# First batch's attention issued from one hand-kept list, with small matmuls ahead of the first MLP

## The chip, the cores and the metric

The kernel runs on one NeuronCore of a Trainium2 chip. The metric is device microseconds (us) of one execution. Five engines with queues of their own work on it: TensorE (PE in the profile, its weight loads PEld), VectorE (DVE), ScalarE (ACT), GpSimd (POOL) and SyncE (SP), which here only issues DMAs. DMAs are issued from the queues of SP, ACT and POOL.

## The reference

Eight batches, 12 heads, 448 positions, 64 elements per head. Attention with normalised queries and keys, then a LayerNorm and an MLP with a residual:

```
q_n, k_n = rmsnorm(q, g_q), rmsnorm(k, g_k)          # over the 64 elements of a head
attn = softmax(q_n @ k_n.T / sqrt(64));  o = attn @ v # [8, 12, 448, 64]
x = o.transpose(0, 2, 1, 3).reshape(8, 448, 768)
xn = (x - mean) / sqrt(var + 1e-6) * g_ln
out = x + relu(xn @ w_ch1) @ w_ch2                    # 768 -> 3072 -> 768
```

All inputs and the output are float32.

## The kernel before, in words

**Stages.** Two heads make a *pair*; a batch has six pairs (p = 0 to 5 in batch 0). Batch 0's attention runs first and alone; then each batch's MLP runs on PE with the next batch's attention cut into small steps between its matmuls (`run`, L560). So only the first attention, with the LayerNorm behind it, has no MLP beside it.

**Units.** q, k and v are loaded and prepared in *units* (L23). Batch 0 has four: unit 0 is pair 0, unit 1 pair 1, unit 2 pairs 2 and 3, unit 3 pairs 4 and 5; unit 4 is the first of batch 1. `prep_ops` (L173) gives the pieces of a unit's preparation, which go over 448 elements per partition for one pair and 896 for two:
- `sk`, `sq`: squares of k and q on ACT (L198); `tk`, `tq`: their sums on DVE (L201)
- `root`: the reciprocal square root of the sums (`_rsqrt`, L47): an addition on DVE (L51), a first guess by an exponential on ACT (L54), then two Newton steps of three tiny DVE instructions each (L57 to L59). `rootq` and `rootk` do one half
- `kg`: k times the product of the two gains, on POOL (L207); `khi`: its float16 part, on POOL for units 1 to 3 (L213), else on ACT (L215); `klo`: the rest, on DVE (L218)
- `qn`, `qdup`: the scaled q in float16 on DVE (L66), and its second copy on DVE (L225) or, for units 2 and 3, POOL
- `vmain`, `vleft` (or `vall`): v in float16, on POOL (L231, L237)

**Per pair.** `trans_k` transposes k on PE into the PSUM tile `tr` and DVE copies it out (L267); `trans_q` does the same for q through the same `tr`, copied out by ACT for pairs 1, 3 and 5 (L281) and by DVE for the others (L283). `scores(p, i)`, i = 0 to 6, are one or two matmuls (L296 to L300) and an exponential on ACT (L302), with two PSUM buffers between. `values(p, i)` are four small matmuls (L325, L327); the last calls `evac_o`, four DVE instructions (L340 to L347). `stats` are the LayerNorm's partial statistics on DVE (L459), every second pair.

**Between attention and MLP.** `ln_ops(0)` (L462): three aggregations (L474), three normalisations `norm` (L479), the LayerNorm's `root`, then for three tiles of tokens a transpose on PE (`ln_trans`, L505) and a copy to `xnT` by ACT (L508, first two) or DVE (L510, third). `run` puts one step of unit 4's preparation after each of these four pieces. The MLP's first matmul is `up` (L523), in 24 chunks of six matmuls and one ReLU on ACT (L525); the second half is `down` (L534).

**Order.** PE, ACT, POOL and SP take their instructions in the order in which the program emits them (`manual_schedule`, L778); on DVE a scheduler decides. What is emitted when in batch 0 comes from `FIRST_ORDER` (L29), rows of (step, unit, pieces): steps -2 and -1 lie ahead of the first scores, step 7p+i goes with `scores(p, i)`; values and transposes of the next pair are spread over the steps by a fixed rule (L398 to L425).

**Loads.** `load_first` (L129) issues q of pair 0 from SP and k of pairs 0 and 1 from ACT's queue, then the rest from SP, with v of pairs 0 and 1 ahead of pairs 2 to 5 of q and k. The weights go from POOL's queue: three parts of w1 (L433) after step 1, two halves of w2 (L438) at step 21.

Of the kernel before, what the change touches and what calls it, by code (L numbers as in the profile page):

```python
# [26 lines left out]
EXP_BIAS = -4.0  # L27

FIRST_ORDER = [  # L29
    (-2, 0, "begin", "sq", "sk", "kg", "tq", "rootq", "tk", "khi", "qn", "qdup", "klo", "rootk"),  # L30
    (-2, 1, "begin", "sk", "sq", "kg", "tk", "tq", "khi"),
    (-1, 1, "root", "klo", "qn", "qdup"),
    (-1, 2, "begin", "sk", "kg", "sq", "tk", "khi"),
    (0, 1, "vall"),
    (0, 2, "tq"), (2, 2, "root"), (4, 2, "klo"), (5, 2, "qn", "qdup"),
    (7, 3, "begin", "sk", "kg"), (9, 3, "sq"), (10, 2, "v"),
    (11, 3, "tk", "khi"), (12, 3, "tq"), (13, 3, "root"), (15, 3, "klo"), (17, 3, "qn", "qdup"),
    (19, 3, "v"),
]
# [7 lines left out]
def _rsqrt(nc, out, a, t, eps, last=None, mul=1.0):  # L47

    eng = nc.vector
    if mul == 1.0:  # L50
        eng.tensor_scalar(out=a, in0=a, scalar1=eps, scalar2=None, op0=ALU.add)  # L51
    else:
        eng.tensor_scalar(out=a, in0=a, scalar1=mul, scalar2=eps, op0=ALU.mult, op1=ALU.add)  # L53
    nc.scalar.activation(out, a.bitcast(INT32), AFT.Exp, scale=-0.5 * LN2 * 2.0 ** -23,  # L54
                         bias=0.5 * LN2 * (127.0 - 0.043))
    for i in range(2):
        eng.tensor_tensor(out=t, in0=out, in1=out, op=ALU.mult)  # L57
        eng.scalar_tensor_tensor(out=t, in0=t, scalar=-0.5, in1=a, op0=ALU.mult, op1=ALU.mult)
        eng.scalar_tensor_tensor(out=last if i and last is not None else out, in0=t, scalar=1.5,  # L59
                                 in1=out, op0=ALU.add, op1=ALU.mult)  # L60

# [13 lines left out]
class _Fast:  # L75
# [53 lines left out]
    def load_first(self):  # L129
        nc = self.nc  # L130
        flat = self.hT.rearrange("p f n -> p (f n)").bitcast(FP32)
        t = [flat[:, 2688 * n:2688 * n + 2688].rearrange("p (w g d) -> p w g d", w=NPAIR, d=D)
             for n in range(2)]
        v = self.p_in.tile([128, 3, 14, D], FP32, tag="qkv", name="vfirst")
        t.append(v.rearrange("p n g d -> p (n g d)").rearrange("p (w g d) -> p w g d", w=NPAIR,
                                                               d=D))
        main = lambda eng, n, p: self.load_main(eng, n, t[n][:, p, 0:6], 0, 2 * p, 2)
        left = lambda eng, n: self.load_left(eng, n, t[n][:, :, 6], 0, 0, H)
        for eng, n in ((nc.sync, 0), (nc.scalar, 1)):
            main(eng, n, 0)  # L140
            left(eng, n)
        main(nc.scalar, 1, 1)
        for n, p in ((0, 1), (2, 0), (2, 1)):
            main(nc.sync, n, p)
        left(nc.sync, 2)
        for p in (2, 4):
            for n in (1, 0):
                for i in range(2):
                    main(nc.sync, n, p + i)
        for p in range(2, NPAIR):  # L150
            main(nc.sync, 2, p)
        self.v_first = t[2]
        for u, (b, hs, m) in enumerate(UNITS):
            if b == 0:
                self.loads[u] = [x[:, hs // 2:hs // 2 + m].rearrange("p w g d -> p (w g) d")
                                 for x in t]
# [16 lines left out]
    def prep_ops(self, u):  # L173
# [28 lines left out]

        def root(n=slice(0, 2)):
            _rsqrt(nc, c["rr"][:, n], c["ssq"][:, n], c["rt"][:, n], D * 1e-6, c["rf"][:, n])
# [6 lines left out]
        def khi():  # L211
            if 0 < u < 4:
                nc.gpsimd.tensor_copy(out=c["khl"][:, :, 0], in_=c["t"][1])  # L213
            else:
                nc.scalar.activation(c["khl"][:, :, 0], c["t"][1], AFT.Identity)  # L215
# [8 lines left out]
        def qdup():  # L224
            (nc.gpsimd if 1 < u < 4 else nc.vector).tensor_copy(out=c["qn"][:, :, 1],  # L225
                                                            in_=c["qn"][:, :, 0])
# [14 lines left out]
        def vall():  # L241

            nonlocal v16, vl, p0
            v16, vl, p0 = self.v16[:, 0:2], self.vl[:, 0:2], 0
            vmain()
            vleft()

        if UNITS[u][0] == 0:
            return dict(begin=begin, sk=lambda: square(1), sq=lambda: square(0), kg=kg, khi=khi,
                        tk=lambda: total(1), tq=lambda: total(0), root=root, klo=klo, qn=qn,  # L250
                        rootk=lambda: root(1), rootq=lambda: root(0), qdup=qdup, vall=vall,
                        v=lambda: (vmain(), vleft()))
        return [lambda: (begin(), square(1), kg()), lambda: total(1), lambda: square(0),
                lambda: (total(0), vmain()), khi, root, klo, None, qn, qdup, vleft]
# [14 lines left out]
    def trans_q(self, p):  # L269
# [3 lines left out]
        ps = self.tr[:, 128:128 + 2 * S].rearrange("p (e s) -> p e s", e=2)  # L273
# [6 lines left out]
        if p in (1, 3, 5):  # L280
            nc.scalar.copy(out=qT, in_=ps.rearrange("p e s -> p (e s)"))  # L281
        else:
            nc.vector.tensor_copy(out=qT, in_=ps.rearrange("p e s -> p (e s)"))  # L283
# [67 lines left out]

    def attention(self):
# [3 lines left out]
        prep = [self.prep_ops(u) for u in range(4)]  # L356

        def at(step, u, *names):
            todo.setdefault(step, []).extend(prep[u][x] for x in names)

        for x in FIRST_ORDER:
            at(*x)
# [10 lines left out]
        todo.setdefault(18, []).append(lambda: self.load_unit(5))  # L373
        todo.setdefault(1, []).append(lambda: [self.load_w1(c, c + 1024) for c in range(0, FF, 1024)])
        todo.setdefault(21, []).append(lambda: [self.load_w2(g) for g in range(2)])
        steps, mark = [], []

        def first():
            self.load_first()
            nc, sh = self.nc, self.sh  # L380
            nc.scalar.activation(sh.warm, sh.ones, AFT.Exp)
            for op in todo.pop(-2):
                op()
            self.trans_k(0)
            self.trans_q(0)
            for op in todo.pop(-1):
                op()
            nc.sync.dma_start(sh.gln, self.g_ln.unsqueeze(0).broadcast_to([128, DM]))
            nc.vector.tensor_scalar(out=sh.gln, in0=sh.gln, scalar1=XS, scalar2=None, op0=ALU.mult)
            self.load_unit(4)  # L390

        def batch(b):
            self.xs[b] = self.p_x.tile([128, 3, DM], FP32, tag="x", name="x")
            if b % 2 == 0:
                self.xls[b // 2] = self.p_xl.tile([128, DM], FP32, tag="xl", name="xl")

        steps.append([first])
        for p in range(n + 1):  # L398
            if p == nb0:
                for x in ((0, 1), (2, 3, 4), (5, 6)):  # L400
                    steps.append([lambda i=i: self.values(nb0 - 1, i) for i in x])
                steps[-1].append(lambda: self.stats(nb0 - 1))
                mark.append(len(steps))
                steps += [[op] for op in self.prep_ops(UNIT_PAIR.index(nb0)) if op is not None]
                steps[-1].append(lambda: self.load_unit(6))
                steps += [[lambda: self.trans_k(nb0)], [lambda: self.trans_q(nb0)]]
            for i in range(7):
                c = []
                if i == 0 and p < n and p % NPAIR == 0:
                    c.append(lambda b=p // NPAIR: batch(b))  # L410
# [3 lines left out]
                if p > 0 and p != nb0:  # L414
                    for x in {0: (), 1: (0, 1)}.get(i, (i,)):
                        c.append(lambda p=p, x=x: self.values(p - 1, x))
                if p > 1 and i == 1 and (p - 1) % NPAIR:
                    c.append(lambda p=p: self.stats(p - 2))
                if p + 1 < n and p + 1 != nb0:
# [42 lines left out]
    def ln_ops(self, b):  # L462
# [23 lines left out]
        def first():  # L486
            aggregate()
            for t in range(3):
                norm(t)
            root()  # L490
# [6 lines left out]
        return [first] + [lambda t=t: trans(t) for t in range(n)]  # L497
# [62 lines left out]
    def run(self):  # L560
        steps, mark = self.attention()
        self.pos = 0

        def upto(target):
            while self.pos < min(target, len(steps)):
                for call in steps[self.pos]:
                    call()
                self.pos += 1

        upto(mark[0])  # L570
        for op in self.ln_ops(0):
            op()
            upto(self.pos + 1)
# [167 lines left out]
def kernel(  # L741
# [35 lines left out]
    with ExitStack() as fctx:  # L777
        with tc.manual_schedule(engines={ENG.PE, ENG.Activation, ENG.Pool, ENG.SP}):  # L778
            _Fast(fctx, tc, sh, q, k, v, moe_g_ln, moe_w_ch1, moe_w_ch2, out).run()
# [34 lines left out]
```

## Time and profile before

| | us |
|---|---|
| median of 8 runs (lowest, highest) | 663.51 (662.71, 664.22) |
| the profiled execution | 663.75 |
| its span | 661.9 |
| PE busy in the span | 618.4 |
| DVE, ACT, POOL busy | 377.3, 358.3, 92.5 |
| first transpose of k (L262) | 12.45 |
| first exponential of scores (L302) | 18.56 |
| last matmul of batch 0's values begins (L327) | 53.48 |
| first matmul of the first MLP (L523) | 62.19 |
| last matmul of the last MLP ends (L534) | 654.69 |

The times in the lower half are starts (or the end) in us from the span's beginning. The profiled execution is 1.9 us longer than its span. A profile row gives an instruction's start, its duration, the engine, the line, the operation with the tiles it writes and reads, and in brackets how long its engine had stood idle and what released it. PEclk, or "granted clock", is the share of full speed that TensorE's clock had.

### The profile page before, as it was taken

To read this page: it belongs to the slowest core of one execution; us is meant where nothing else is said; L and a number is where in the kernel's file an instruction comes from. 1 tells how busy PE (TensorE), PEld (TensorE's weight loads), DVE (VectorE), ACT (ScalarE), POOL (GpSimd) and SP (SyncE) were. 2 spreads that over 40 slices of the span, in tenths; PEclk is the share of its full clock that TensorE was granted. 3 is DMA by queue.
4 is the path that set the end of the run, shared out by engine and by line. 5 is a ranking of instruction groups with operands and counts; after the bars stand their busy time and mean duration, and the time that the engine had idled before them with its cause. 6 is when DMAs were issued, how large, how long until landed. Compare 5 with 4: busy or idle time off the path is not lost.

```text
span 661.9 us, 12501 instructions
## 1 busy us (share of the span) xinstructions
PE 618.4 (93%) x5066; PEld 380.7 (58%) x5066; DVE 377.3 (57%) x890; ACT 358.3 (54%) x641; POOL 92.5 (14%) x113
## 2 busy tenths in 40 slices
PE   0676999999999999999999999999999999999995
PEld 0453566655566666655566666655566666654563
DVE  5878778855556566765456666865356553380011
ACT  2694787547843477527754377617764287304300
POOL 2732222120220201201220012202201020000000
PEclk9997999999999999999999999999999999999998
DMA  7999944042030433032130241112331100010011
GB/s 208 244 216 214 222 139 110 4 156 83 3 108 25 130 87 85 25 103 73 41 108 25 83 132 53 58 58 77 83 85 50 48 2 1 25 49 1 0 49 51
DMA packets 71824, 54.81 MB, mean 83 GB/s; under 512 B 22736, under 2 KB 65744, under 8 KB 71760
## 3 DMA queue, kind: packets, MB, share of 16 engines
q1 hardware_dynamic: 61600, 43.86, 22.6%
q0 software_dynamic: 8528, 9.44, 8.4%
q8 instruction: 41, 0.67, 0.4%
q10 hardware_dynamic: 1632, 0.66, 0.4%
q14 instruction: 23, 0.19, 0.1%
HBM read 52.36 MB, written 11.01 MB: 96 GB/s over the span
## 4 chain that ended last, share of the span: by engine, by line
PE 83%; DVE 8%; ACT 4%; DMA 2%; issue 1%; SPq 1%; ACTq 0%; DVEq 0%
PE psH L523 31%; PE psC L534 30%; PE psS L296 7%; PE oA L325 4%; PE tr L278 2%; PE tr L265 2%; DVE xn L479 2%; ACT E L302 2%; PE oB L327 1%; PE psS L299 1%; PE psS L300 1%; PE psX L505 1%; DVE stat L459 1%; DMA hT<-in_k_dram 1%; DMA hT<-in_q_dram 1%
## 5 line engine op out<-in xcount | busy, mean ns | idle before, releaser
L302 ACT ACTIVATE E<-psS,rr_all 128x448 f16<-128x448 f32 x336 | 208.4, 634 | 80.5 <-PE psS L296 65.3
L523 PE MATMUL psH<-xnT,w 128*128 128x512 f16 (+1 forms) x1152 | 247.2, 355 | 1.8 <-ACT xnT L508 1.8
L534 PE MATMUL psC<-w,hT 128*128 128x384 f16 x1344 | 241.5, 326 | 1.9 <-DVE x L538 1.9
L525 ACT ACTIVATE hT<-psH 128x384 f16<-128x384 f32 (+1 forms) x192 | 104.7, 545 | 117.3 <-PE psH L523 114.8
L534 PEld LDWEIGHTS <-hT 128*128 128x128 f16 x1344 | 125.0, 98 | 73.1 <-issue 2.4
L523 PEld LDWEIGHTS <-w 128*128 128x128 f16 x1152 | 106.3, 98 | 86.7 <-issue 5.7
L296 PE MATMUL psS<-qT,kT 128*128 128x448 f16 x288 | 103.0, 360 | 7.7 <-ACT E L302 5.7
L207 POOL TENSOR_TENSOR qkv<-qkv,gprod 128x896 f32<-128x896 f32 x21 | 43.8, 2084 | 418.2 <-issue 301.8
L325 PEld LDWEIGHTS <-E 128*128 128x128 f16 x1008 | 72.1, 98 | 49.6 <-issue 3.9
L538 DVE SCALAR_TENSOR_TENSOR x<-psC,rs_all,x 128x384 f32<-128x384 f32 x48 | 29.5, 615 | 74.8 <-PE psC L534 74.4
L325 PE MATMUL oA<-v,E 128*128 128x65 f16 x864 | 67.3, 194 | 0.0
L267 DVE COPY kT<-tr 128x960 f16<-128x960 f16 x48 | 31.5, 655 | 45.2 <-PE tr L265 44.6
L327 PE MATMUL oB<-v,E 128*128 128x65 f16 x288 | 52.3, 194 | 0.0
L283 DVE COPY qT<-tr 128x896 f16<-128x896 f16 x45 | 28.0, 623 | 35.4 <-PE tr L278 35.0
L296 PEld LDWEIGHTS <-kT 128*128 128x128 f16 x288 | 28.5, 100 | 22.6 <-issue 3.6
L340 DVE RECIPROCAL rec_all<-oA 128x6 f32<-128x6 f32 x48 | 9.4, 196 | 55.2 <-PE oA L325 55.1
L201 DVE TENSOR_REDUCE ssq<-qn 128x14 f32<-128x896 f32 (+1 forms) x25 | 26.2, 1046 | 11.7 <-ACT qn L198 10.6
L327 PEld LDWEIGHTS <-E 128*128 128x128 f16 x336 | 32.6, 97 | 0.1
L218 DVE TENSOR_TENSOR khl<-qkv,khl 128x896 f16<-128x896 f32 x21 | 22.9, 1093 | 16.4 <-ACT khl L215 16.2
L54 ACT ACTIVATE stat<-stat 128x3 f32<-128x3 int32 (+1 forms) x8 | 1.7, 209 | 50.8 <-DVE stat L53 50.8
L201 DVE TENSOR_REDUCE ssq<-khl 128x14 f32<-128x896 f32 (+1 forms) x25 | 26.1, 1046 | 4.3 <-ACT khl L198 3.6
L342 DVE TENSOR_TENSOR x<-oA,rec_all 128x384 f32<-128x384 f32 x48 | 26.8, 558 | 1.5
(89 smaller groups left out, 540.0 us busy)
## 6 DMA issues: line engine op xcount, KB each, us to landing
out_dram<-x SPq DMA_DIRECT2D x24, 384.0 KB, 2.3
qkv<-in_k_dram SPq DMA_DIRECT2D x21, 384.0 KB, 3.3
qkv<-in_q_dram SPq DMA_DIRECT2D x21, 384.0 KB, 3.9
qkv<-in_v_dram SPq DMA_DIRECT2D x21, 384.0 KB, 4.4
w<-in_moe_w_ch_dram POOLq DMA_DIRECT2D x3, 1536.0 KB, 17.7
w<-in_moe_w_ch_dram POOLq DMA_DIRECT2D x2, 2304.0 KB, 32.3
out_dram<-xl SPq DMA_DIRECT2D x8, 192.0 KB, 3.2
qkv<-in_k_dram SPq DMA_DIRECT2D x42, 32.0 KB, 3.3
```

The lines of the kernel that those rows point to most:

```text
L201: nc.vector.tensor_reduce(out=c["ssq"][:, n], in_=c["sq", n], axis=AX.X, op=ALU.add)
L207: nc.gpsimd.tensor_tensor(out=c["t"][1], in0=c["t"][1], in1=sh.gprod.unsqueeze(1).broadcast_to([128, g, D]), op=ALU.mult)
L267: nc.vector.tensor_copy(out=kT.rearrange("p g d -> p (g d)"), in_=ps[:, 0:960])
L283: nc.vector.tensor_copy(out=qT, in_=ps.rearrange("p e s -> p (e s)"))
L296: nc.tensor.matmul(ps[:, 0:S], kT[:, 192 + 128 * i:320 + 128 * i], qT[:, h * S:(h + 1) * S], start=True, stop=True)
L302: nc.scalar.activation(out=c["E"][:, i], in_=ps[:, 0:S], func=AFT.Exp, scale=self.rr[:, 1, g:g + 1], bias=EXP_BIAS)
L325: nc.tensor.matmul(oA[:, t, cs], E[:, i, ts(t, 128)], rhs, start=(i == 0 and t == 0), stop=(i == 6 and t == 2))
L327: nc.tensor.matmul(oB[:, cs], E[:, i, 320:448], rhs, start=(i == 0), stop=(i == 6))
L523: nc.tensor.matmul(ps[:, 0:N], sh.w1[:, dc, ts(f, 128)], xnT[:, dc, 0:N], start=(dc == 0), stop=(dc == NDC - 1))
L525: nc.scalar.activation(out=hT[:, f, 0:N], in_=ps[:, 0:N], func=AFT.Relu)
L534: nc.tensor.matmul(ps[:, 0:384], hT[:, f, ts(t, 128)], sh.w2[:, f, ts(g, 384)], start=(f == 0), stop=(f == NFF - 1))
L538: nc.vector.scalar_tensor_tensor(out=x[:, ts(g, 384)], in0=ps[:, 0:384], scalar=self.rs[:, b, t:t + 1], in1=x[:, ts(g, 384)], op0=ALU.mult ...
```

## The change

1. `FIRST_ORDER` and the step rule for batch 0 are replaced by `ORDER`, one list of pieces for all of batch 0, emitted by `first_attention`. In an entry the first letter is the piece and the last digit the unit: b begin, c and a the squares of q and k, e and d their sums, f the addition, g the guess, h the Newton steps (fq/fk, gq/gk, hq/hk: one half), i kg, j khi, k klo, l qn, m qdup, v the copies of v. K, Q, T are `trans_k`, `trans_q` and `stats` of a pair; S and V are `scores` and `values`; L loads a unit, W a part of the weights, G loads the LayerNorm's gain and G2 scales it.
2. Until the LayerNorm of batch 0 is emitted, DVE too follows the program's order; afterwards its scheduler decides again.
3. `_rsqrt` is split into addition, guess and Newton steps, which stand apart in the list.
4. `trans_q` of batch 0 uses PSUM buffers of its own (`psQ`, from the three that the MLP uses) and no longer `tr`; ACT copies pair 0, DVE pairs 1 to 5 (before: ACT 1, 3, 5). `qdup` of unit 2 moves from POOL to DVE.
5. `load_first` issues everything from SP, in the order q, k of pair 0, then q and k up to pair 3, then v.
6. After batch 0's values, 22 matmuls of 384 columns into an unused tile `psW`. In `ln_ops(0)` the `root` goes behind the transposes, and unit 4's preparation is no longer put between its pieces: it starts inside the first MLP.

From the later part of the first MLP on, the order of instructions on every engine is that of before.

```diff
+WARM = 22
+POOL_HI, POOL_DUP, ACT_Q = (1, 2, 3), (3,), (0,)
+ORDER = """
+b0 c0 e0 fq0 gq0 a0 hq0 i0 d0 fk0 gk0 j0 b1 c1 a1 i1 l0 m0 k0 hk0 d1 K0 e1 j1 Q0 f1 S0.0 g1 h1
+k1 l1 m1 b2 a2 i2 G L4 W0 c2 S0.1 v0 S0.2 d2 K1 S0.3 j2 Q1 S0.4 W1 S0.5 W2 e2 S0.6 f2 g2 h2
+V0.0 S1.0 k2 l2 m2 S1.1 b3 S1.2 a3 S1.3 i3 V0.1 V0.2 V0.3 v2 K2 S1.4 V0.4 S1.5 Q2 c3 V0.5 S1.6
+V0.6 S2.0 T0 S2.1 e3 d3 V1.0 V1.1 S2.2 V1.2 j3 S2.3 V1.3 V1.4 f3 g3 V1.5 S2.4 K3 h3 Q3 k3 S2.5
+l3 S2.6 V1.6 v3 m3 L5 G2 S3.0 S3.1 V2.0 K4 V2.1 W3 S3.2 S3.3 V2.2 V2.3 S3.4 V2.4 Q4 S3.5 V2.5
+S3.6 V2.6 K5 S4.0 S4.1 T1 Q5 V3.0 V3.1 S4.2 V3.2 S4.3 V3.3 S4.4 V3.4 S4.5 V3.5 S4.6 V3.6 S5.0
+V4.0 V4.1 T3 S5.1 S5.2 V4.2 S5.3 V4.3 S5.4 V4.4 W4 S5.5 V4.5 V4.6 V5.0 V5.1 S5.6 V5.2 V5.3
+V5.4 V5.5 V5.6 T5
+""".split()
...
-        for eng, n in ((nc.sync, 0), (nc.scalar, 1)):
-            main(eng, n, 0)
-            left(eng, n)
-        main(nc.scalar, 1, 1)
-        for n, p in ((0, 1), (2, 0), (2, 1)):
+        for n in range(2):
+            main(nc.sync, n, 0)
+            left(nc.sync, n)
+        for n, p in ((1, 1), (0, 1), (1, 2), (1, 3), (0, 2), (0, 3), (2, 0), (2, 1)):
             main(nc.sync, n, p)
         left(nc.sync, 2)
...
-        ps = self.tr[:, 128:128 + 2 * S].rearrange("p (e s) -> p e s", e=2)
+        tr = self.ps_m.tile([128, 1024], FP16, tag="mlp", name="psQ") if p < NPAIR else self.tr
+        ps = tr[:, 128:128 + 2 * S].rearrange("p (e s) -> p e s", e=2)
...
-        if p in (1, 3, 5):
+        if p in ACT_Q:
             nc.scalar.copy(out=qT, in_=ps.rearrange("p e s -> p (e s)"))
...
             for t in range(3):
                 norm(t)
-            root()
+            if b:
+                root()
...
-        return [first] + [lambda t=t: trans(t) for t in range(n)]
+        return [first] + [lambda t=t: trans(t) for t in range(n)] + ([] if b else [root])
...
+        self.first_attention()
+        ps = self.ps_m.tile([128, 512], FP32, tag="mlp", name="psW")
+        for _ in range(WARM):
+            nc.tensor.matmul(ps[:, 0:384], self.sh.id16,
+                             self.v16.rearrange("p s h j d -> p (s h j d)")[:, 0:384],
+                             start=True, stop=True)
         for op in self.ln_ops(0):
             op()
-            upto(self.pos + 1)
...
-        with tc.manual_schedule(engines={ENG.PE, ENG.Activation, ENG.Pool, ENG.SP}):
-            _Fast(fctx, tc, sh, q, k, v, moe_g_ln, moe_w_ch1, moe_w_ch2, out).run()
+        manual = {ENG.PE, ENG.Activation, ENG.Pool, ENG.SP}
+        with tc.manual_schedule(engines=manual | {ENG.DVE}):
+            fast = _Fast(fctx, tc, sh, q, k, v, moe_g_ln, moe_w_ch1, moe_w_ch2, out)
+            fast.run_first()
+        with tc.manual_schedule(engines=manual):
+            fast.run_rest()
```

## The prediction

> **What bounds the kernel now.** I read the busy slices of the page first: PE is at 9 in nearly all of them, and the few low ones lie at the start. The table by stage says the same (columns: window, its length, then busy us of PE, PEld, DVE, ACT and POOL with instruction counts, granted clock, DMA share, GB/s):
>
> ```profile
> 57.70:62.20 4.50, 2.48 (x19) 1.79 (x20) 4.00 (x7) 2.55 (x5) 1.31 (x1) 0.50 1.26 217
> 62.20:66.80 4.60, 4.60 (x15) 2.15 (x15) 4.50 (x8) 2.69 (x5) 2.06 (x4) 0.51 1.32 204
> 66.80:70.00 3.20, 3.20 (x26) 2.06 (x24) 2.76 (x10) 1.50 (x4) 0.00 (x0) 1.00 1.32 205
> 150.00:250.00 100.00, 99.29 (x826) 61.26 (x825) 56.98 (x133) 60.25 (x109) 13.16 (x15) 1.00 0.25 72
> ```
>
> Once the MLPs run, PE is 99% busy. So what the change is worth is the time at which the first MLP matmul starts (62.19 us), plus the clock at which it runs: in the second row 15 matmuls take 4.60 us at clock 0.51, 0.307 each, where six take 0.97 us later (0.162 each).
>
> Second, the chain of waits from the last values to that matmul:
>
> ```profile
> 54.07 0.20 DVE rec_all L340
> ...
> 55.41 1.08 DVE stat L459 x3
> 56.49 0.33 DVE stat L474 x3
> 56.82 2.72 DVE xn L479 x3
> ...
> 59.97 0.69 issue
> 60.65 1.49 ACT xnT L508 x2
> 62.15 0.04 issue
> 62.19 7.26 PE psH L523 x30
> ```
>
> Here see that ACT's two copies end it. They stood behind the LayerNorm's guess (L54, 59.65) and a square of unit 4 (59.80 to 60.75), though their transposes began at 57.74.
>
> Third, what PE waits for in batch 0's attention:
>
> ```profile
> PE tr L262 <- DVE khl L218: 12.4, 1, 12.4
> PE psS L296 <- ACT E L302: 5.2, 9, 2.3
> PE tr L275 <- DVE qn L225: 4.3, 2, 3.0
> ```
>
> DVE and ACT set the pace there, not PE. ACT has 42 exponentials (24.2 us busy, spaced 0.54 when they run back to back), yet they spread from 18.56 to 53.2. DVE is nearly full from 10 to 25 us, and part of that is waiting inside instructions. The timeline shows it, POOL first, DVE below:
>
> ```profile
> 17.31 2.08 POOL L207 TENSOR_TENSOR hT<-hT,gprod 128x896 f32<-128x896 f32 x1 [2.59 <-DMA vfirst<-in_v_dram]
> 17.86 1.56 DVE L58 SCALAR_TENSOR_TENSOR rt<-rt,ssq 128x14 f32<-128x14 f32 x1
> ```
>
> A Newton instruction that takes 0.15 elsewhere takes 1.56 and ends with POOL's kg. The same happened at kg of units 0 and 1 and khi of unit 3: 0.46, 0.95, 1.40 and 0.59 us lost. Sums (L201) and copies out of PSUM beside POOL kept their times (1.07, 0.62).
>
> **The change, part by part.** All against the profiled execution, 663.75 (span 661.9 and 1.85 around it); that is 0.24 above the median.
>
> *Start.* ACT's DMA issue at 6.81 held its table load (7.22) and so the first square to 8.63. Those issues go to SP, so q's square can start when q lands, about 7 us. DVE is held to 7.55 by the gains' product (L766 to L770). From there: sum of q 0.6, addition and guess 0.35, six Newton instructions at 0.20 (1.2), sum of k 0.55, addition 0.16 with 0.4 of holding by kg0: 10.9. Then qn and qdup 0.85, klo 0.6 (12.35); the k half's six Newton steps 1.2 plus 1.05 held by kg1 (1.13 long, starting about 12.7, behind the square of unit 1): 14.65. Sum of unit 1 0.55, copy of kT 0.6: 15.8. q's transposes have their own PSUM and ACT's copy (0.9) is done by then. First exponential 0.57 later (as 17.99 to 18.56): **16.4** instead of 18.56. SP's eighth issue waits for the first landing, as it did before (idle 2.69 to 4.69), so k may land up to 0.7 earlier or later; both ends go into the range.
>
> *Units 1 and 2.* The guess of unit 1 stands on ACT behind the first exponential (16.95), and Newton, klo, qn of unit 1 wait behind it on DVE. The square of k of unit 2 follows that guess, so kg2 starts 1.18 later (18.13), after five Newton steps, and holds the last one, klo and qn until 20.2: 1.85 lost. klo, qn, qdup 1.5; sum 1.0; kT, qT 1.2: 23.85. Sum of q, addition 1.2; the guess of unit 2 comes behind the last exponential of pair 0 at 25.3; Newton 1.55, klo and qn 2.15: 29.0. Here kg3 becomes ready while qn runs, and stands against qdup (0.4), which has moved to DVE. If POOL goes first it costs 2.1, if DVE does, 0. The four kg of before cost 0.46, 0.95, 1.40 and 0, 0.70 on the mean; I take 1.0. qdup, kT, qT 1.6: 31.65, and pair 2's exponentials start at 32.1.
>
> *Units 3 to the end of attention.* On DVE until qT of pair 4: evacuation 1.35, sums 2.0, addition, kT, Newton, qT 2.6, klo and qn 2.1, evacuation, gain, kT, qT 3.0: 42.7. From there ACT sets it: 0.45 to the first exponential, 14 of 0.54 (7.55), 0.35 for the last values: **51.05** instead of 53.70. The copies of qT for pairs 3 and 5 that move to DVE are in this sum (0.55 each); the second (by 47) is hidden by pair 4's exponentials. POOL loses one qdup (0.93). Gain 2.65; with no holding at all 47.5 (then ACT and PE at half clock bound it), with every kg in full 52.7.
>
> *LayerNorm.* Evacuation 1.35 at once (before: 0.37 late, behind pair 4's), statistics 1.0, aggregation 0.33, three norms 2.8, last transpose and DVE's copy 1.05, wake-up 0.05: MLP at 51.05 + 6.6 = 57.65, against 8.49 us from 53.70 to 62.19. ACT's copies are earlier than DVE's now, because guess and squares stand behind them. Gain 1.9. Sum with attention: **4.55**.
>
> *Small matmuls.* 22 of 0.162 are 3.6 us, hidden by the 3.7 until the first norm is done. At half clock they would take 6.8 and delay the transposes by 3.1. Before, clock 0.5 lasted from 56.5 (2.8 after the last matmul) to 66.75. With them, PE is without matmuls other than transposes for about 3.0 us. If the clock stays up, 15 matmuls take 2.44 instead of 4.60: gain **2.15**, otherwise 0. The idle part before the fall was 2.8 without any transposes; 1 us of these lies in the new gap, so I take 2.15.
> [...]
>
> *Unit 4's preparation inside the MLP.* Two squares (0.95 each), two sums (1.07 each), kg now compete with the first ReLUs. First scores of pair 6 come after 10 chunks, not 7. PE idled 1.13 in 70 to 80 for such pieces. From -0.3 (that idling eases) to 1.9 (both squares uncovered): I take **0.4** lost, near the row.
>
> *Weights.* The last part of w1 landed at about 51 (25.4 + 25.6) and is used by the 17th chunk; halves of w2 at 66.8 and 81.6, first used at 103.5. POOL issues w1 at about 20 and 25 now (23.6 before), w2 at about 40: nothing.
>
> Forecast: 663.75 - 4.55 - 2.15 + 0.4 = **657.4**.
>
> **Rivals.**
> 1. *POOL and DVE do not meet.* The order keeps kg beside sums and copies; attention ends at 47.5. For: before, kg3 cost nothing. Against: kg2 follows its square directly. 663.75 - 6.2 - 1.9 - 2.15 + 0.4 = 653.9.
> 2. *The clock falls all the same* in the gap with only transposes. 657.4 + 2.15 = 659.6.
> 3. *The list does not shorten attention* (DVE in fixed order waits for guesses behind exponentials as long as it waited before): end at 53.7, 663.75 - 1.9 - 2.15 + 0.4 = 660.1.
> 4. *Slower: the fixed order on DVE meets all of POOL's work.* POOL has 14.2 us in batch 0 (kg 6.4, khi 2.4, v 4.4, qdup 0.9); I charge 4.3. If the other 9.9 held DVE too, attention would end at 60.95 and the time be 667.3. It is slower by over 0.2% from 7.7 of these 9.9 on. Against it: before, 3.4 of some 15 were lost.
>
> **How the numbers follow.** Chances: forecast 0.45, rival 1 0.17, rival 2 0.20, rival 3 0.10, rival 4 0.08. The forecast alone spans 655.5 to 659.5 (kg3 and its neighbours, landing of k, unit 4). The range to rivals 1 to 3 is 653.3 to 661.5. A measurement of this kernel tells 0.2% (1.3 us) from no change. Faster 0.88: all but rival 4 and the part of rivals 2 and 3 that come together (662.2), which with a small rival 4 gives 0.05 for the same; slower 0.07.
>
> **What would show it.** First exponential near 16.4; DVE instructions of Newton or klo beside kg2 stretched by up to 2 us; the last values ending near 51; first MLP matmul 6.6 later, with the DVE copy ending its wait; clock 1.00 in the first 5 us of the MLP. I am wrong if attention ends after 53.7, if the clock shows 0.5 there, or if PE idles over 2 us in the first ten chunks.

## The result and the profile after

The changed kernel takes 666.09 us (median of 11 executions, 664.66 to 668.18) against 663.50 for the kernel before on the same chip (32 executions): ratio 1.0043 (95% interval 1.0034 to 1.0051). It is **slower** by 2.9 us by the ratio (2.6 by the medians), where 657.4 was forecast. Its profiled execution took 665.45 (span 663.6), 1.70 more than that of before; the sums below go by these two.

| us from the start | before | forecast | after |
|---|---|---|---|
| first exponential | 18.56 | 16.4 | 16.95 |
| first exponential of pair 2 | 34.35 | 32.1 | 35.94 |
| first exponential of pair 4 | 44.39 | 43.15 | 47.82 |
| last values of batch 0 end | 53.70 | 51.05 | 56.51 |
| first MLP matmul | 62.19 | 57.65 | 63.27 |
| first store of the output | 134.00 | | 135.71 |
| last MLP matmul ends | 654.69 | | 656.42 |

Behind the first store (issued when the first MLP is done) the kernels run alike: 520.69 and 520.71 us. The loss arises before it: 1.61 gained at the start, 4.42 lost from the first exponential to the last values, 1.73 gained in the LayerNorm, 0.63 lost in the first MLP.

The table by stage of the changed kernel, the same three stretches as before, shifted with the first MLP matmul (columns: window, length, busy us of PE, PEld, DVE, ACT, POOL, granted clock, DMA share, GB/s):

```profile
58.40:63.30 4.90, 3.24 (x30) 1.86 (x28) 4.19 (x10) 1.67 (x3) 0.00 (x0) 1.00 1.32 205
63.30:67.90 4.60, 4.60 (x29) 2.78 (x30) 2.96 (x8) 3.55 (x7) 2.05 (x2) 1.00 1.31 205
67.90:71.10 3.20, 3.20 (x26) 1.98 (x25) 2.82 (x8) 2.33 (x5) 2.23 (x4) 1.00 1.32 205
```

The second row now holds 29 matmuls at clock 1.00, where it held 15 at 0.51: the small matmuls did what they were to do in this execution. The timeline of the same kernel, from the LayerNorm's transposes to the first MLP matmul (in brackets the idle time before an instruction, and what ended it):

```profile
60.70 1.73 ACT L520 COPY xnT<-psX 128x768 f16<-128x768 f16 x2 [4.65 <-PE psX L517]
62.56 0.56 DVE L522 COPY xnT<-psX 128x768 f16<-128x768 f16 x1 [0.60 <-PE psX L517]
...
63.26 6.99 PE L535 MATMUL psH<-xnT,w 128*128 128x384 f16 x42 [0.74 <-DVE stat L69]
```

ACT's copies no longer end this chain: they are done at 62.43, and what comes last is the DVE copy (62.56 to 63.12; the profile names the small DVE instruction after it). So the LayerNorm's step held. Two other views show the loss. What PE waited for in batch 0's attention:

```profile
PE tr L278 <- DVE khl L233: 17.2, 4, 13.2
PE psQ L292 <- DVE qn L240: 2.0, 2, 1.3
PE psS L313 <- DVE qT L300: 1.7, 1, 1.7
PE psS L313 <- DVE kT L283: 1.5, 1, 1.5
PE psS L313 <- ACT E L319: 1.1, 4, 0.3
```

Before, 5.2 us of PE's waits there were for ACT's exponentials; now it is 1.1, and four rows name DVE. And the timeline of POOL and DVE:

```profile
18.60 2.07 POOL L222 TENSOR_TENSOR hT<-hT,gprod 128x896 f32<-128x896 f32 x1 [2.17 <-ACT khl L206]
18.77 1.94 DVE L63 SCALAR_TENSOR_TENSOR rr_all<-rt,rr 128x14 f32<-128x14 f32 x1
...
21.16 1.78 DVE L77 SCALAR_TENSOR_TENSOR qn<-hT,rr_all 128x448 f16<-128x448 f32 x1
...
21.62 0.84 POOL L246 CAST v<-vfirst 128x768 f16<-128x768 f32 x1
22.39 1.07 POOL L252 CAST vl<-vfirst 64x128 f16<-64x128 f32 x2
...
25.30 1.64 POOL L444 DMA_DIRECT2D w<-in_moe_w_ch_dram  x2
26.38 0.56 DVE L212 TENSOR_SCALAR ssq<-ssq 128x28 f32<-128x28 f32 x1
...
29.91 2.99 POOL L222 TENSOR_TENSOR hT<-hT,gprod 128x896 f32<-128x896 f32 x1 [2.97 <-ACT khl L206]
31.00 2.15 DVE L240 COPY qn<-qn 128x896 f16<-128x896 f16 x1
```

A Newton instruction of 0.17 takes 1.94 beside unit 2's kg, qn of unit 1 (0.62 elsewhere) takes 1.78 beside the copies of v, and qdup of unit 2 (0.39) takes 2.15 beside unit 3's kg, which itself takes 2.99 instead of 2.08. The addition of unit 2 (L212, 0.17 elsewhere) stands beside no POOL computation, but beside POOL's issue of two loads of w1, and ends with it at 26.94: 0.39 lost. With kg of units 0 and 1 (0.89, 0.97) and the copies of v of unit 3 (0.64), DVE lost 7.6 us; before it lost 3.4.

What PE waited for in the first MLP, from its first matmul to 104:

```profile
PE tr L292 <- DVE qn L240: 1.8, 1, 1.8
PE psS L313 <- ACT E L319: 1.2, 2, 0.6
PE tr L292 <- DVE kT L283: 0.9, 1, 0.9
```

The kernel before has none over 0.7 behind its first MLP matmul.

### The profile page after: what moved, and what is told of

Its sections match the earlier page's. It is cut to its first block, busy times and chain, and to the rows that moved or that the text cites. A ratio compares the mean times of both kernels' runs of the same rounds, so it can differ in the third digit from the quotient of the medians.

```text
span 663.6 us, 12533 instructions
## 1 busy us (share of the span) xinstructions
PE 621.6 (94%) x5088; PEld 382.3 (58%) x5088; DVE 383.4 (58%) x893; ACT 357.2 (54%) x639; POOL 93.5 (14%) x112
## 4 chain that ended last, share of the span: by engine, by line
PE 79%; DVE 11%; issue 4%; ACT 2%; DMA 1%; POOL 1%; SPq 0%; DVEq 0%; ACTq 0%; POOLq 0%
PE psH L535 29%; PE psC L546 29%; PE psS L313 7%; PE oA L342 4%; PE tr L295 2%; PE tr L281 2%; DVE xn L490 2%; PE oB L344 1%; DVE qn L77 1%; PE psS L316 1%; PE psS L317 1%; DVE khl L233 1%; DVE stat L470 1%; PE psX L517 1%; ACT E L319 1%
## 5 line engine op out<-in xcount | busy, mean ns | idle before, releaser
L535 PE MATMUL psH<-xnT,w 128*128 128x512 f16 (+1 forms) x1152 | 244.7, 352 | 0.7 <-DVE stat L69 0.7
L342 PE MATMUL oA<-v,E 128*128 128x65 f16 x864 | 67.8, 196 | 0.0
L300 DVE COPY qT<-tr 128x896 f16<-128x896 f16 x42 | 26.2, 623 | 33.9 <-PE tr L295 33.7
L278 PE MATMUL tr<-id,khl 128*128 128x128 f16 x48 | 10.8, 225 | 17.2 <-DVE khl L233 17.2
```

The lines of the kernel that those rows point to most:

```text
L342: nc.tensor.matmul(oA[:, t, cs], E[:, i, ts(t, 128)], rhs, start=(i == 0 and t == 0), stop=(i == 6 and t == 2))
L535: nc.tensor.matmul(ps[:, 0:N], sh.w1[:, dc, ts(f, 128)], xnT[:, dc, 0:N], start=(dc == 0), stop=(dc == NDC - 1))
```

## The experiments

Two theories stood against each other for the attention. **H:** the order of the list sets POOL's work beside those DVE instructions that it holds. **F:** a fixed order on DVE loses by itself, because DVE waits for what stands ahead (guesses, PSUM). For the first MLP: **U**, PE waits for unit 4's preparation, against **C**, the clock does not stay up. All ratios are to the kernel before on the same chip.

### POOL's products moved in the list

`e1_late_kg` is the changed kernel with the squares of k and kg of units 2 and 3 later (POOL's order stays as it was, so the copies of v come later too), so that kg runs beside sums and PSUM copies:

```diff
-k1 l1 m1 b2 a2 i2 G L4 W0 c2 S0.1 v0 S0.2 d2 K1
+k1 l1 m1 b2 c2 S0.1 S0.2 a2 i2 G L4 W0 v0 d2 K1
-S1.1 b3 S1.2 a3 S1.3 i3 V0.1 V0.2 V0.3 v2 K2 S1.4 V0.4 S1.5 Q2 c3 V0.5
+S1.1 S1.2 S1.3 V0.1 V0.2 V0.3 K2 S1.4 V0.4 S1.5 Q2 b3 c3 a3 i3 v2 V0.5
```

> The changed kernel with the same pieces, but the squares of k of units 2 and 3 (and with them kg on GpSimd) stand later in the list: a2 and i2 behind S0.2, a3 and i3 behind c3. Theory H (GpSimd's kg, and the copies of v behind it, hold VectorE's two-operand instructions, which in a fixed order lie on the path): the stretched Newton step (1.94), qn (1.78) and qdup (2.15) go back to 0.2, 0.6 and 0.4, attention ends near 52.5 to 53.5 instead of 56.5, the time falls by 2.5 to 4 to 662 to 663.5. Rival F (the fixed order itself, waiting for guesses behind exponentials): no gain, 666 or up to 0.5 more.

Measured: 663.00, ratio 0.9999 (0.9988 to 1.0010), 3.1 less than the changed kernel (2.9 by the ratios); the attention ends at 53.53 instead of 56.51. The same instructions in its timeline:

```profile
18.79 0.17 DVE L63 SCALAR_TENSOR_TENSOR rr_all<-rt,rr 128x14 f32<-128x14 f32 x1
...
19.41 0.62 DVE L77 SCALAR_TENSOR_TENSOR qn<-hT,rr_all 128x448 f16<-128x448 f32 x1
...
20.51 2.09 POOL L222 TENSOR_TENSOR hT<-hT,gprod 128x896 f32<-128x896 f32 x1 [4.06 <-DMA gln<-in_moe_g_ln_dram]
...
29.19 0.39 DVE L240 COPY qn<-qn 128x896 f16<-128x896 f16 x1
```

All three are back at their own times, with the same DVE order. H holds; F alone can't give this. Added up in the same way, DVE's holds are 4.5 us here, 3.1 less than in the changed kernel, and the attention ends 3.0 earlier. Two things came along and are not separated from this: ACT takes two exponentials of pair 0 ahead of unit 2's square of k, and PE's matmuls of scores take 0.35 instead of 0.56 from 31.8 on, in the changed kernel only from 39.5 on.

### POOL's products left out

```diff
-                        e=lambda: total(0), f=eps, g=guess, h=root, i=kg, j=khi, ...
+                        e=lambda: total(0), f=eps, g=guess, h=root, i=lambda: None, j=khi, ...
```

> The changed kernel without POOL's products of k with the gains in units 0 to 3 (these multiplications are left out). In the changed kernel DVE lost 0.89, 0.97, 1.77 and 1.76 us beside them, 5.4 together. If these holds are what failed in the attention's step: its end moves from 56.5 to 51 (50.5 to 52), near the 51.05 forecast, and the time to about 661. If DVE's fixed order waits for something else (guesses behind exponentials, late squares): attention ends at 53.5 or later and the time is 663 or more.

Measured: 660.75, ratio 0.9963 (0.9949 to 0.9977); the attention ends at 51.21, 5.30 earlier than in the changed kernel, where DVE lost 5.4 beside these products. So the four kg as a whole cost the attention 5.3 us; leaving them out also shortens the chain kg, khi, klo, so this is not the hold alone. Nor does it say that nothing else failed. The forecast had charged them with 4.3, and without any holds it would have ended at 47.5 (bound by ACT and PE), not at 51.2. DVE still loses about 2.3 here (unit 2's addition takes 0.61 for 0.17, a Newton instruction of unit 3 0.73 for 0.19), where POOL has the copies of v, khi, a qdup and its issue of weight loads left. The rest stays open; in this execution the granted clock was at 0.50 from 25.9 to 29.2 and from 36.1 to 39.4, inside the attention.

### DVE left to its scheduler

```diff
-        with tc.manual_schedule(engines=manual | {ENG.DVE}):
+        with tc.manual_schedule(engines=manual):
```

> The changed kernel with VectorE's order given back to its scheduler in batch 0; list, loads, PSUM of q and small matmuls stay. If VectorE's fixed order (H or F) is what lost the time in attention, attention ends near the 53.7 of before or earlier, time 662.5 to 664. Rival: the loads, the PSUM of q or the copies moved to VectorE lost it: 665.5 to 666.5.

Measured: 668.66 (4 executions), ratio 1.0075 (1.0058 to 1.0092): slower still, and outside both cases. qdup of unit 2 beside unit 3's kg takes 1.58 instead of 2.15, but the scheduler puts klo of unit 3 behind statistics that only the LayerNorm needs. Its timeline:

```profile
41.97 1.08 DVE L470 BATCH_NORM_STATS2 stat<-x 128x6 f32<-128x256 f32 x3
42.97 1.07 DVE L233 TENSOR_TENSOR khl<-hT,khl 128x896 f16<-128x896 f32 x1
...
44.10 0.29 PE L278 MATMUL tr<-id,khl 128*128 128x128 f16 x1 [4.06 <-DVE khl L233]
...
45.66 1.89 ACT L319 ACTIVATE E<-psS,rr_all 128x448 f16<-128x448 f32 x3 [4.73 <-PE psS L313]
```

ACT stands for 4.73 us, and pair 4 begins at 50.02 instead of 47.82. The granted clock was also at 0.50 here from 42.3 to 49.0, from within PE's wait of 4.06 on; its share of the 2.2 is not separated. With this list, then, giving DVE's order back to the scheduler gains nothing: that the fixed order alone lost the time is not borne out.

### The copies of qT

`e7_late_kg_act` is the kernel with late kg and `ACT_Q = (0, 3, 5)`.

> The changed kernel with POOL's products moved (as in the run with late kg) and, besides, the copies of qT of pairs 3 and 5 given back to ACT. If DVE's full load is what still bounds the attention, its end moves from 53.5 to about 52.4 (two copies of 0.55) and the time from 663.0 to about 662. If ACT's exponentials bound it there, ACT gains 1.1 us of work and the time is 663.0 to 664.

Measured: 662.35, ratio 0.9980 (0.9972 to 0.9989), which meets the first time, but not its reason: the attention ends at 53.41 instead of 53.53, with a first exponential that is 0.33 earlier, so the copies gave nothing there. Of its 11 executions 10 had a mean granted clock of 0.996 or 0.997; with late kg alone it was 4 of 10, and these four took 662.3 to 662.4. So the difference of the medians goes with the clock; why it fell more seldom stays open.

### The small matmuls

`e4_no_warm` is the changed kernel with `WARM = 0`; `e5_before_warm` is the kernel before with the 22 small matmuls behind batch 0's values.

> The changed kernel without the 22 small matmuls. If they keep the clock up: clock 0.5 returns in the first microseconds of the MLP and the time is 667.8 to 668.5. Rival: the gap is short enough without them, or they cost what they bring: 665.8 to 666.3.

> The kernel before with one part of the change alone: the 22 small matmuls behind the last values of batch 0. Theory A (the clock's gain adds to the rest): the clock stays up in most executions, 15 matmuls take 2.4 instead of 4.6 us, time 2.15 lower, about 661.3. Theory B (the first MLP then waits for unit 4's preparation, which a slow start of the MLP had hidden in part): first scores of pair 6 move by less than 1.2 us, time 662.2 to 662.8.

Measured for `e4_no_warm`: 667.66 (4 executions), ratio 1.0072 (1.0055 to 1.0088), just under its first range, with the clock at 0.50 from 59.9 to 66.7. So the small matmuls are worth 1.6 us in the changed kernel (1.9 by the ratios); but in the kernel before (`e5_before_warm`) the time is 663.06, ratio 0.9996 (0.9988 to 1.0005): nothing. PE's timeline shows the difference, first of the changed kernel, then of `e5_before_warm`:

```profile
56.34 3.74 PE L586 MATMUL psW<-v,id 128*128 128x384 f16 x22
...
63.26 1.46 PE L535 MATMUL psH<-xnT,w 128*128 128x384 f16 x8 [0.74 <-DVE stat L69]
```

```profile
53.46 3.74 PE L573 MATMUL psW<-v,id 128*128 128x384 f16 x22
...
62.10 2.72 PE L523 MATMUL psH<-xnT,w 128*128 128x384 f16 x8 [2.08 <-ACT xnT L508]
```

From the end of the small matmuls to the MLP there are 3.2 us with nothing but transposes in the first, 4.9 in the second, and there eight matmuls take 2.72 instead of 1.46. Its table by stage has the fall 3.5 us into the gap:

```profile
57.20:60.69 3.49, 1.53 (x19) 1.01 (x18) 3.15 (x8) 1.12 (x3) 0.00 (x0) 1.00 1.23 225
60.69:67.52 6.83, 5.42 (x18) 2.58 (x19) 6.05 (x13) 4.15 (x7) 3.37 (x4) 0.50 1.32 203
```

So neither theory of that expectation was the point: the clock just did not stay up.

### The LayerNorm in the kernel before

`e6_before_ln_warm` is the kernel before with the small matmuls and with the LayerNorm's `root` behind the transposes; unit 4's preparation stays between the pieces.

> The kernel before with its own attention, with the small matmuls and with the LayerNorm's root moved behind the transposes; unit 4's preparation stays between the LayerNorm's pieces. If the attention's order was the only loss of the change: LayerNorm 8.5 to about 7.7 (as where the preparation was put between the pieces), clock 1.5 to 2.1, time 660.5 to 661.5. If unit 4's chain eats both: 662.5 or more, with PE idle over 3 us between the first MLP matmul and the first scores of pair 6.

Measured: 663.72, ratio 1.0002 (0.9993 to 1.0010): the second case by its time. LayerNorm 8.16; the gap behind the small matmuls is 4.6 us, and the clock is at half from 62.27, 0.6 after the first MLP matmul, to 65.68; PE waits 1.2 us longer in the first MLP than before.

### Unit 4's preparation

Two runs move its start: `e3_prep_ln` puts one step of it behind each LayerNorm piece of the changed kernel, as before; `e8_late_kg_prep` issues its squares and its kg ahead of the small matmuls, in the kernel with late kg.

```diff
         for op in self.ln_ops(0):
             op()
+            self.upto(self.pos + 1)
```

> The changed kernel with one step of unit 4's preparation put back after each piece of the first LayerNorm, as before. Theory P (its square, kg, khi, klo, qn, qdup chain starts too late inside the MLP and TensorE waits for the transposes and scores of pair 6): TensorE's idle time from 62 to 105 falls from 4.8 to about 2, time 663.3 to 664. Rival: that idle time has another cause (weights, two squares in ACT's queue): 666, or more, since the square and a sum lengthen the LayerNorm by up to 1.

```diff
         self.first_attention()
+        for j in (0, 2):
+            for call in self.steps[j]:
+                call()
+            self.steps[j] = []
```

> The changed kernel with POOL's products moved and, besides, unit 4's two squares and its kg issued ahead of the small matmuls, so that the chain to pair 6 starts some 4 us earlier. If PE's waits of 4.8 us in the first MLP come from that chain: they fall to about 2, time 660.7 to 661.5, with up to 0.5 lost in the LayerNorm (DVE's sum of k ahead of its copy). If they come from elsewhere: time 663 or more.

Measured for `e3_prep_ln`: 666.00 (4 executions), ratio 1.0045 (1.0028 to 1.0062), no gain: the LayerNorm takes 7.75 instead of 6.76, since DVE's sum of k now stands ahead of its copy, and this eats what the first MLP gains (71.52 instead of 72.44). For `e8_late_kg_prep`: 664.77, ratio 1.0022 (1.0010 to 1.0033), worse by 1.8 than with late kg alone (1.5 by the ratios). Its LayerNorm takes 7.75 too; its profiled execution is the slowest of the eleven, with the clock at half from 61.3 to 68.1. The timeline of `e8_late_kg_prep`, unit 4's chain alone:

```profile
54.95 2.08 POOL L222 TENSOR_TENSOR qkv<-qkv,gprod 128x896 f32<-128x896 f32 x1 [9.18 <-ACT khl L206]
...
69.56 0.94 ACT L230 ACTIVATE khl<-qkv 128x896 f16<-128x896 f32 x1
...
70.54 1.09 DVE L233 TENSOR_TENSOR khl<-qkv,khl 128x896 f16<-128x896 f32 x1 [6.31 <-ACT khl L230]
...
74.89 0.23 PE L292 MATMUL tr<-id,qn 128*128 128x128 f16 x1 [1.46 <-DVE qn L240]
```

kg is done at 57.0 (in the changed kernel at 67.9), but khi follows at 69.56: in ACT's order it stands behind the ReLUs of the chunks that are emitted before it, and q's transposes stand only six MLP matmuls behind those of k, as in the changed kernel. An early start of kg alone does not help where both ends of the rest are tied to places in PE's order. What can be changed is that distance.

### More MLP matmuls between the transposes

`e9_fill` is `e7_late_kg_act` with two empty steps; `e11_fill_more` has three there and one behind `trans_q`:

```diff
-steps += [[lambda: self.trans_k(nb0)], [lambda: self.trans_q(nb0)]]
+steps += [[lambda: self.trans_k(nb0)], [], [], [lambda: self.trans_q(nb0)]]
```

> The run with late kg and qT copies on ACT, and in the first MLP two empty steps between the transposes of k and of q of pair 6, so that PE has two more MLP chunks to do while unit 4's chain ends. If PE's idle 1.75 ahead of q's transposes comes only from the place where they stand in PE's order: that wait goes to under 0.3, time 662.35 - 1.5 = 660.9 (660.5 to 661.5). If the wait only moves to the scores or the exponentials behind it: within 0.5 of 662.35.

> As the run with two empty steps, with three between the transposes of k and of q and one more ahead of the first scores. If what is left of PE's waits in the first MLP (0.59 and 0.62 ahead of scores) comes from the place too: another 0.5 to 1 less, 660.0 to 660.9. If those waits are for ACT's exponentials beside unit 5's squares: no less than with two, 660.9 to 661.5.

Measured: 661.16, ratio 0.9965 (0.9953 to 0.9977), for `e9_fill`, and 660.99, ratio 0.9963 (0.9950 to 0.9977), for `e11_fill_more`: no difference between the two. Both beat both kernels: the kernel before by 2.2 and 2.4 us, the changed one by about 5. `e9_fill` lies by its time where its first case put it, though the wait did not go under 0.3; `e11_fill_more` lies at the border of its two. PE's waits in the first MLP of `e9_fill`:

```profile
PE psS L313 <- ACT E L319: 1.6, 3, 0.6
PE tr L292 <- DVE qn L240: 0.8, 1, 0.8
```

q's transposes (12 MLP matmuls behind those of k, no longer six) wait 0.8 instead of 1.8, and the wait for kT one pair later (0.6 in `e7_late_kg_act`, 0.9 in the changed kernel) is gone. The waits for exponentials stay. U holds, in a sharper form: PE waited because the transposes stood too early in its order.

The same edit in the kernel before with its own attention (`e6_before_ln_warm` and two empty steps):

> The kernel before with its own attention, the small matmuls, the LayerNorm's root moved behind the transposes, and two empty steps between the transposes of k and q of pair 6. If the gains of clock and LayerNorm were eaten by PE's waits for unit 4's chain (0.75 ahead of q's transposes, 0.59 and 0.36 ahead of scores, 0.85 ahead of the next pair's transposes, where this run has no empty steps): time falls from 663.7 to 662.2 to 662.8. If they were lost elsewhere: 663.3 or more.

Measured: 664.17, ratio 1.0002 (0.9993 to 1.0011), the case against. The wait ahead of q's transposes did go (0.75 to none in its row), but the gap behind the small matmuls was 4.6 us, and the clock was at half to 67.02. The length of the first MLP differs among all these kernels by two things, PE's waits and the clock. The rows by stage, from the first MLP matmul to the first store, in the order before, after, `e9_fill`, `e11_fill_more`, `e12_before_ln_fill`; 606 matmuls in each:

```profile
62.19:134.00 71.81, 69.73 (x606) 44.75 (x606) 57.12 (x130) 50.64 (x93) 15.58 (x20) 0.97 0.56 121
```

```profile
63.27:135.71 72.44, 67.73 (x606) 44.04 (x607) 57.52 (x132) 51.38 (x95) 17.82 (x20) 1.00 0.48 108
```

```profile
60.62:131.38 70.76, 67.59 (x606) 44.00 (x607) 56.89 (x132) 51.09 (x95) 17.78 (x20) 1.00 0.58 125
```

```profile
61.26:131.60 70.34, 67.69 (x606) 43.91 (x607) 57.13 (x132) 50.87 (x95) 17.80 (x20) 1.00 0.57 123
```

```profile
61.95:134.61 72.66, 69.83 (x606) 44.91 (x607) 55.73 (x132) 49.79 (x93) 13.50 (x16) 0.97 0.57 120
```

Length less PE's busy time is what PE stood: 2.08, 4.71, 3.17, 2.65, 2.83. A us at half clock costs 0.47 (15 matmuls took 4.60, at full clock 2.44); there were 4.56, 0, 0, 0 and 5.07 of them. Length less both is 67.6, 67.7, 67.6, 67.7 and 67.4, and for `e3`, `e4`, `e5` and `e6` 67.6, 67.8, 67.6 and 67.7. So the changed kernel won 2.1 by the clock and lost 2.6 to PE's waits.

## Why the prediction was wrong

Forecast was 6.3 less, measured in the profile 1.7 more: 8.0 apart.

- **Start: right.** 16.95 for 16.4. SP's eighth issue did not wait for a landing, against the forecast: SP has no wait for a DMA in the first 16 us. In the kernel before, it was the fourth issue that stood, for 2.0 us.
- **Attention: failed, 5.5 of the 8.0.** The step was "51.05 instead of 53.70"; it ended at 56.51. Term by term: 0.55 from the start. Up to qT of pair 1 another 0.95: kg of unit 2 held DVE by 1.77, as forecast (1.85), but the copies of v behind it held qn by another 1.16, which had not been charged. Up to pair 2 another 2.35: the forecast took 1.0 between 0 and 2.1 for unit 3's kg and it cost 1.76, POOL's issue of weight loads held the addition by 0.39, and the rest of 1.2 lies between qdup and the first exponential, where the forecast put 1.65 (kT, qT, 0.45) and the trace has 2.8. Then 0.83 to pair 4, 0.64 of it the copies of v of unit 3 beside Newton steps, and 0.78 in the last two pairs.
- In sum, DVE's holds were 7.6 where 4.3 were charged; "I take 1.0", drawn from the mean (0.70) of four holds of another order, was the wrong way to price the fifth: DVE's order was fixed, so what stands beside what could be read from the list. That leaves 2.2 of the 5.5, and its cause stays open. Only a companion is known: PE's matmuls of scores stayed longer at 0.56 us, before they went to 0.35. Two rows of PE's timeline in the changed kernel show the step:

```profile
38.23 0.56 PE L313 MATMUL psS<-qT,kT 128*128 128x448 f16 x1
...
39.47 0.35 PE L313 MATMUL psS<-qT,kT 128*128 128x448 f16 x1
```

  Before, the same matmul takes 0.56 at 31.29 and 0.36 at 32.62. How much of the 2.2 that is was not tried. Two pairs of runs with the same list for the attention give a measure. `e9_fill` and `e11_fill_more` start their first exponential at 17.07; in the second the clock was at half again from 25.8 to 32.6 and from 39.5 to 42.8, and its attention ends 0.65 later. `e8_late_kg_prep`, at half from 27.1 to 33.9 and from 40.8 to 44.1, ends it 0.95 after `e1_late_kg`.
- **LayerNorm: right.** 6.76 for 6.6, with DVE's copy as its end.
- **Clock: right in the profiled execution, 2.1 for 2.15.** But the clock differed between executions: seven of the changed kernel had a mean clock of 0.995 to 0.997 and took 664.7 to 666.1, four had 0.986 to 0.992 and took 666.9 to 668.2. The profiled one is among the fast ones, and the medians lie further apart (2.6) than the profiles (1.7). Where the clock fell in those four no trace shows. In the profiled executions of `e10_no_kg` and `e11_fill_more`, with the same gap and a mean of 0.991, it fell inside the attention and not at the MLP, so rival 2 is not shown to have come true.
- **Unit 4's preparation: failed, 2.2 of the 8.0.** "From -0.3 to 1.9, I take 0.4": it was 2.6, beyond its upper bound. The forecast had priced ACT's squares beside the ReLUs. What cost time was PE's own order: first scores moved from behind 36 MLP matmuls to behind 54, and yet q's transposes stood six of them (1.0 us) behind k's, while Newton, qn, the copy of kT and qdup, which follow klo on DVE, take 3.3 us (70.03 to 73.32). In the kernel before, this chain began during the LayerNorm, and PE was at half clock for the first 4.6 us of the MLP; its qdup is done at 69.71, and q's transposes run at 70.65 without a wait. Both things helped, by the time that PE stood in the first MLP: 2.08 before; 3.93 with the early start and full clock (`e3_prep_ln`); 4.42 with the late start and half clock for the first 2.8 us (`e4_no_warm`); 4.71 in the changed kernel, with neither. The empty steps took back 1.2 to 1.8 of this (4.40 in `e7_late_kg_act`, 3.17 in `e9_fill`, 2.65 in `e11_fill_more`).
- **Rival 4** named the right mechanism for the attention (POOL's work holds DVE) and the right sign, at 0.08; that the order on DVE was fixed is not shown to be what did it. Its point of decision was wrong: it called for 7.7 us of uncharged holds, when 3.3 of them were enough together with PE's waits in the MLP.

## What to carry to other kernels

When an order is fixed by hand, lay the two engines' lists side by side and charge every pair that will meet, instead of a mean of past meetings; here a shift of two products by a few places came to 3 us. An engine that gets faster (a clock kept up, an earlier start) gains only as much as the chain beside it can follow: ask where in its order the first instruction stands that needs that chain, and put independent work ahead of it. Judge a gain of the clock over several executions and not from one profile.

## What the runs showed of the hardware

- The hold goes both ways: unit 3's kg on POOL began at 29.91 beside DVE's qn (29.88 to 30.97) and took 2.99 us, 0.91 over its own 2.08, and the copy qdup behind qn ended at 33.15, 0.25 after kg. DVE's sums (1.08, 1.09) beside kg of units 2 and 3 and its copies out of PSUM (0.65, 0.61) beside unit 2's kg kept their times in `e1_late_kg`. Held were instructions with two inputs in SBUF (the Newton instruction with 1.94, qn with 1.78) and with one (the copy qdup with 2.15; the addition with 0.56, beside POOL's issue of weight loads). The addition took 0.61 in `e10_no_kg` as well (21.89 to 22.50). What decides which instruction is held was not shown.
- Without other matmuls than transposes, the clock fell in four of the five profiled executions with a gap of 4.2 to 4.9 us between the small matmuls and the MLP (`e5`, `e6`, `e8`, `e12`; not in `e3`), and in one of seven with a gap of 3.2 (`e2`), in `e2` and `e6` 0.6 after the MLP had begun. It also fell inside the attention in `e2`, `e4`, `e8`, `e10` and `e11`, between 25.8 and 42.8. Once down, it stayed at half for 3.41 us (as in `e6`, 62.27 to 65.68), 6.83 (as in `e5`, 60.69 to 67.52) or 10.24 (the kernel before, 56.51 to 66.75), which is once, twice and three times 3.41; and the same list for the attention kept it in `e9_fill` and lost it twice in `e11_fill_more`. The view of the clock has a blind spot: it says 1.00 for the attention of the changed kernel, where the same matmul takes 0.56 at 38.23 and 0.35 at 39.47. Why the clock fell in some executions and stayed up in others with the same gap was not shown.
